# Attention, Fourier mixing and a feed-forward layer on one core: the second feed-forward product of the last three chunks as seven quarter products

## The chip, the core and the metric

One core of a Trainium2 chip runs the whole program. The metric is the device time of one execution in microseconds; lower is better. The engines are TensorE (PE in the profile; its weight loads are PEld), VectorE (DVE), ScalarE (ACT), GpSimd (POOL) and SyncE (SP), which here only starts transfers.

## What is computed

Eight sequences of 576 tokens, 8 heads of 64. All is float32.

```
a    = softmax(phi)                      # phi: 8, 8, 576, 32
k_m  = a^T k ;  v_m = a^T v              # 32 memory slots per head
attn = softmax(q k_m^T / 8) v_m
x    = heads side by side                # 8, 576, 512
u    = x + real(fft over tokens and over the 512 features of x)
un   = (u - mean) / sqrt(var + 1e-6)
out  = u + max(un @ w_ch1, 0) @ w_ch2    # w_ch1 512 x 2048, w_ch2 2048 x 512
```

## The kernel before

The 4608 tokens are 36 tiles of 128, taken in 18 chunks of two tiles (`CH = 2`). A generator, `background`, makes the rows of u of each batch: pooling weights, memories, scores, spectrum and the mixes (`mix_m`, `mix_x`, `add_mix`), which write u into a ring of eight tiles. `advance` runs it some steps further while the ring has room. `norm_chunk` normalises a chunk (ScalarE, VectorE, GpSimd), splits it into two float16 parts in `ud` and turns it with a transposing transfer on SP.

The feed-forward layer of a chunk goes in eight units (`NW = 8`), each of 256 hidden features (`UB = 2` blocks of 128). Float32 factors are two float16 parts, a high and a low one, and a product is three matmuls: high by high, high by low, low by high.

- `ffn1(c, unT, j, hs)` is the first product of a unit: 2 blocks x 4 x 3 = 24 matmuls of 256 columns (two tiles of 128 tokens), issued by the helper at line 288, into one PSUM bank `ph` (two buffers). ScalarE writes the high part of max(., 0) to the ring `hring` (line 864), VectorE the low part (line 865).
- `ffn2(c, j, hs, po)` is the second product: 2 blocks x 2 token tiles x 3 = 12 matmuls of 512 columns (line 874), with the hidden activations as the stationary operand and `w2s` as the moving one, added over all units into two PSUM banks `po`, one per token tile (pool `ps2`, two buffers).
- `finish(c, po)` adds u to each of the two banks on VectorE (line 886) and writes the tile out on SP (line 887).

The main loop goes over n, the units of chunks 1 to 17 in order: `ffn2` of unit n, then `run_ffn1(n + NHS)`, which emits first products up to seven units ahead (`NHS = 7`), then a step of the background; after a chunk's last unit `finish`, then the background until the tiles of chunk c + 2 are made, then the norm of chunk c + 2. This is the order of emission. A planner puts the instructions of each engine into their final order: it takes what was emitted earlier first, and what is emitted later where the earlier can't run yet by its own timing of the kernel. On the chip each engine then works through its list in order.

Of the buffers, `stg`, `rawt`, `phs`, `et`, `aeo`, `attnT`, `aring`, `vh`, `at` and `elt` belong to the background; after its last step they are not used.

Of the kernel before, what the change touches and what calls it, by code (L numbers as in the profile page):

```python
# [10 lines left out]
F32 = mybir.dt.float32  # L11
F16 = mybir.dt.float16
# [3 lines left out]
AF = mybir.ActivationFunctionType  # L16
ALU = mybir.AluOpType
# [3 lines left out]
P = 128  # L21
B, H, S, D, M = 8, 8, 576, 64, 32
NG = H // 2
DM = H * D
# [13 lines left out]
CH = 2  # L38
NU = 8
NHS = 7  # L40
# [8 lines left out]
BN = 2  # L49
UB = 2  # L50
NW = NF // UB
UW = UB * DM
EB = 14
L2 = [2, 4, 6]
# [4 lines left out]

HEADS = [0, 1, 2, 3, 7, 6, 5, 4]
SLOT = np.concatenate([np.arange(256), 511 - np.arange(256)])

# [69 lines left out]
def kernel(  # L134
# [39 lines left out]
    cout = small[:, 713:714]  # L174
# [17 lines left out]
    hring = const.tile([P, NW, 2, 4, P], F16, name="hring")  # L192
# [24 lines left out]
        nc.gpsimd.memset(t, 0.0)  # L217
    scratch = const.tile([P, 400], F32, name="scratch")
    share = const.tile([P, 2 * NJ], F32, name="share")
    rings, taken = {}, [0]  # L220

    def tiny(tag, n, bufs=2):
# [603 lines left out]
    def h_slot(c, j):  # L826
        return hring[:, (4 + c * NW + j) % NW]

# [17 lines left out]
    def ffn1(c, unT, j, hs):  # L846

        ph = ps1.tile([P, UB, CH, P], F32, tag="h", name=f"ph_{c}_{j}")
        mm = groups()
        for f in range(UB):  # L850
            i = 0
            for k in range(NK):
                for lw, lu in ((0, 0), (0, 1), (1, 0)):
                    mm(
                        ph[:, f],
                        lhsT=w1t[:, j, lw, k, f * P : (f + 1) * P],
                        rhs=unT[:, lu, :, k],
                        start=(i == 0),
                        stop=(i == 3 * NK - 1),
                    )  # L860
                    i += 1
        h = h_slot(c, j)
        phv = ph.rearrange("p f t c -> p (f t) c")
        nc.scalar.activation(h[:, 0], phv, AF.Relu)  # L864
        nc.vector.scalar_tensor_tensor(  # L865
            out=h[:, 1], in0=phv, scalar=0.0, in1=h[:, 0], op0=ALU.max, op1=ALU.subtract
        )
        hs.append(h)

    def ffn2(c, j, hs, po):  # L870
        for f in range(UB):
            for t in range(CH):
                for i, (lh, lw) in enumerate(((0, 0), (0, 1), (1, 0))):
                    nc.tensor.matmul(  # L874
                        po[t],
                        lhsT=hs[j][:, lh, f * 2 + t],
                        rhs=w2s[:, j * UB + f, lw, :],
                        start=(j == 0 and f == 0 and i == 0),
                        stop=(j == NW - 1 and f == UB - 1 and i == 2),
                    )  # L880

    def finish(c, po):
        for t in range(CH):
            idx = CH * c + t
            u = us.pop(idx)
            nc.vector.scalar_tensor_tensor(out=u, in0=po[t], scalar=cout if c else 0.5, in1=u, op0=ALU.mult, op1=ALU.add)  # L886
            nc.sync.dma_start(out=out[idx], in_=u)
# [110 lines left out]
    marks = {}  # L998
    us = {}
    n_tiles = B * S // P  # L1000
    n_chunks = n_tiles // CH
# [171 lines left out]
    def run_ffn1(upto):  # L1173
        nonlocal ahead
        while ahead < min(upto, n_steps):
            c, j = divmod(ahead, NW)
            ffn1(c, unTs[c], j, hs[c])
            ahead += 1
# [4 lines left out]
    for n in range(NW, n_steps):  # L1183
        c, j = divmod(n, NW)
        if j == 0:
            po = [ps2.tile([P, 512], F32, tag="o", name=f"po_{c}_{t}") for t in range(CH)]
        ffn2(c, j, hs[c], po)
        run_ffn1(n + NHS)
        if j < NW - 1:
            advance(CH * c, steps=1)  # L1190
        else:
            finish(c, po)
            if c + 2 < n_chunks:
                advance(CH * (c + 1), CH * (c + 3))
                unTs[c + 2] = norm_chunk(c + 2)


# [62 lines left out]
```

## Time and profile before

| | us |
|---|---|
| median of 3 runs | 943.62 (942.4 to 962.26) |
| the profiled execution | 943.25 |
| its span, first to last instruction | 941.4 |
| TensorE busy | 931.6 |
| VectorE busy | 548.0 |
| ScalarE busy | 459.6 |
| GpSimd busy | 217.5 |

The span is what the profile shows; the execution's own time is 1.85 us longer. Matmuls are pipelined and their ends are modelled, so what one matmul costs is read from how many stand in a stretch of known length, and not from the duration of one (379 ns for one of 512 columns). Lines of the kernel are given as L874.

### The profile page before, as it was taken

What the parts mean: (1) busy time and instruction counts of PE and PEld (TensorE: products, weight loads), DVE (VectorE), ACT (ScalarE), POOL (GpSimd) and SP (SyncE); (2) the same over time, 40 slices, a digit from 0 to 9 for tenths busy, and PEclk for the clock granted to TensorE, in tenths of its full rate; (3) what the DMA queues carried; (4) which work ended last, traced back from release to release, by engine and by line L of the source; (5) the groups of instructions that cost most, each with busy time, mean ns of one, the idle gap of its engine ahead of it and who ended that gap; (6) DMA issues with size and microseconds to landing.
All of it is one profiled execution on the core that took longest, in us unless ns stands there. A gap on an engine that the chain in (4) does not pass through costs nothing.

```text
span 941.4 us, 18994 instructions
## 1 busy us (share of the span) xinstructions
PE 931.6 (99%) x7820; PEld 666.2 (71%) x7820; DVE 548.0 (58%) x1271; ACT 459.6 (49%) x920; POOL 217.5 (23%) x255
## 2 busy tenths in 40 slices
PE   9999899999999999999999999999999999999998
PEld 8977577676777777676767767777776767666664
DVE  5989957576656666667514766667656675221111
ACT  5668858655465536554514554656446444311110
POOL 1313424142212314223100331323122231200000
PEclk9999899999999999999999999999999999999999
DMA  9957521642235412553104531373124211110000
GB/s 328 383 217 245 184 85 24 124 123 68 53 75 123 105 42 46 141 111 93 24 23 86 115 103 42 59 162 98 26 68 85 72 25 47 23 46 23 1 24 22
DMA packets 115959, 88.09 MB, mean 94 GB/s; under 512 B 100384, under 2 KB 100384, under 8 KB 113824
## 3 DMA queue, kind: packets, MB, share of 16 engines
q1 hardware_dynamic: 115872, 86.87, 34.7%
q8 instruction: 61, 1.00, 0.4%
q14 instruction: 26, 0.21, 0.1%
HBM read 58.15 MB, written 9.44 MB: 72 GB/s over the span
## 4 chain that ended last, share of the span: by engine, by line
PE 88%; DVE 3%; ACT 1%; issue 1%; POOL 0%; DVEq 0%; ACTq 0%
PE ph L288 38%; PE po L874 37%; PE pm L288 2%; PE pp_t L288 2%; PE px_t L288 2%; PE psc L288 1%; PE po L838 1%; PE pa L684 1%; DVE w2s L930 1%; PE ph L821 1%; PE pv L657 1%; PE pp_t L727 1%; PE pf L362 1%; DVE w1t L930 0%; ACT elt L941 0%
## 5 line engine op out<-in xcount | busy, mean ns | idle before, releaser
L288 PE MATMUL ph<-unring,w1t 128*128 128x256 f16 x3264 | 388.9, 273 | 0.0
L874 PE MATMUL po<-w2s,hring 128*128 128x512 f16 x1632 | 378.8, 379 | 0.0
L288 PEld LDWEIGHTS <-w1t 128*128 128x128 f16 x3264 | 315.0, 98 | 64.4 <-issue 3.3
L874 PEld LDWEIGHTS <-hring 128*128 128x128 f16 x1632 | 156.8, 98 | 158.0 <-issue 0.4
L865 DVE SCALAR_TENSOR_TENSOR hring<-ph,hring 128x512 f16<-128x512 f32 x136 | 93.1, 685 | 155.4 <-ACT hring L864 154.8
L864 ACT ACTIVATE hring<-ph 128x512 f16<-128x512 f32 x136 | 80.3, 591 | 161.3 <-PE ph L288 160.9
L592 POOL TENSOR_TENSOR aring<-aring,scratch 128x384 f32<-128x384 f32 x28 | 23.3, 833 | 212.2 <-DVE scratch L590 208.6
L787 POOL TENSOR_TENSOR scratch<-scratch,small 128x1 f32<-128x1 f32 x36 | 21.7, 608 | 168.2 <-DVE scratch L786 135.1
L288 PEld LDWEIGHTS <-stg 128*128 128x128 f16 x1152 | 44.8, 98 | 8.4
L586 ACT ACTIVATE aring<-aring,scratch 128x384 f32<-128x384 f32 x24 | 14.7, 612 | 71.0 <-DVE aring L585 71.0
L808 POOL TENSOR_TENSOR ud<-un,ud 128x1024 f16<-128x1024 f32 x17 | 36.2, 2129 | 29.6 <-ACT ud L807 27.7
L509 POOL TENSOR_TENSOR stg<-rawt,stg 128x640 f16<-128x640 f32 x12 | 17.7, 1475 | 90.2 <-ACT rawt L508 90.2
L838 PE MATMUL po<-w2s,hring 128*128 128x512 f32 x64 | 32.8, 637 | 4.3 <-ACT hring L824 4.2
L611 ACT CAST aeo<-eo 128x384 f16<-128x384 f32 x30 | 15.3, 511 | 41.4 <-DVE eo L608 41.4
L886 DVE SCALAR_TENSOR_TENSOR uring<-po,small,uring 128x512 f32<-128x512 f32 x34 | 24.0, 742 | 17.6 <-PE po L874 17.6
L576 DVE TENSOR_REDUCE scratch<-psc 128x12 f32<-128x384 f32 x32 | 17.6, 549 | 28.5 <-PE pm L288 16.1
L763 DVE SCALAR_TENSOR_TENSOR uring<-px_t,scratch,share 128x256 f32<-128x256 f32 (+1 forms) x80 | 33.9, 475 | 0.2 <-PE px_t L288 0.2
L602 POOL TENSOR_TENSOR aring<-aring 128x128 f32<-128x128 f32 x56 | 32.8, 605 | 2.1
L604 DVE TENSOR_TENSOR eo<-aring 128x128 f32<-128x128 f32 x29 | 29.5, 1018 | 5.9 <-POOL aring L602 5.9
L288 PE MATMUL pm<-et,stg 128*128 128x64 f16 (+1 forms) x740 | 32.0, 195 | 0.0
L821 PE MATMUL ph<-unring,w1t 128*128 128x256 f32 x128 | 32.0, 395 | 0.0
L749 DVE SCALAR_TENSOR_TENSOR share<-pp_t,scratch,small 128x257 f32<-128x257 f32 (+1 forms) x48 | 21.0, 480 | 18.1 <-ACT small L746 18.0
(263 smaller groups left out, 1212.3 us busy)
## 6 DMA issues: line engine op xcount, KB each, us to landing
out<-uring SPq DMA_DIRECT2D x36, 256.0 KB, 2.1
rawt<-in_raw SPq DMA_DIRECT2D x13, 640.0 KB, 4.9
stg<-in_raw SPq DMA_DIRECT2D x13, 640.0 KB, 4.8
stg<-in_w SPq DMA_DIRECT2D x7, 1024.0 KB, 6.0
rawt<-in_raw SPq DMA_DIRECT2D x15, 384.0 KB, 3.3
stg<-in_raw SPq DMA_DIRECT2D x15, 384.0 KB, 3.1
phs<-in_raw SPq DMA_DIRECT2D x28, 160.0 KB, 3.8
w2s<-in_w SPq DMA_DIRECT2D x4, 1024.0 KB, 10.8
```

The source lines that it names most:

```text
L288: m = nc.tensor.matmul(out, lhsT=lhsT, rhs=rhs, start=start, stop=stop)
L592: eng.tensor_tensor(out=a, in0=a, in1=sm.unsqueeze(2).to_broadcast([P, 12, M]), op=ALU.mult)
L602: eng.tensor_tensor(out=a2[:, i : i + 4], in0=a[:, 0:4], in1=a[:, 4:8], op=op)
L604: nc.vector.tensor_tensor(out=eo[:, 1:3, 0], in0=ap[:, 1:3, 0], in1=ap[:, 1:3, 1], op=ALU.add)
L763: nc.vector.scalar_tensor_tensor(out=u[rows, hs], in0=px[rows, hs], scalar=igx[rows], in1=tm[rows, w * NJ + half : w * NJ + half + 256], o ...
L808: marks[f"ul{c}"] = nc.gpsimd.tensor_tensor(out=ud[:, 1], in0=un, in1=ud[:, 0], op=ALU.subtract)
L821: nc.tensor.matmul(ph, lhsT=w[:, k, f * P : (f + 1) * P], rhs=unTs[0][:, k], start=(k == 0), stop=(k == NK - 1))
L838: nc.tensor.matmul(po[t], lhsT=h[:, f, t], rhs=w[:, f], start=(j == 0 and f == 0), stop=(j == NW - 1 and f == UB - 1),)
L864: nc.scalar.activation(h[:, 0], phv, AF.Relu)
L865: nc.vector.scalar_tensor_tensor(out=h[:, 1], in0=phv, scalar=0.0, in1=h[:, 0], op0=ALU.max, op1=ALU.subtract)
L874: nc.tensor.matmul(po[t], lhsT=hs[j][:, lh, f * 2 + t], rhs=w2s[:, j * UB + f, lw, :], start=(j == 0 and f == 0 and i == 0), stop=(j == NW ...
L886: nc.vector.scalar_tensor_tensor(out=u, in0=po[t], scalar=cout if c else 0.5, in1=u, op0=ALU.mult, op1=ALU.add)
```

## The change

In chunks 15, 16 and 17 (`C0 = 15`) the second product of a unit, a 2 x 2 block matrix of activations (two token tiles by two hidden blocks) by a 2 x 2 block matrix of weights (two hidden blocks by two halves of 256 output columns), is made from seven block products in place of eight (Winograd's form of Strassen's scheme). Every product is three float16 matmuls of 256 columns, so 21 in place of 12 of 512.

- `ffn1_sums` takes the place of the two activations in `ffn1`: ScalarE writes the four blocks in float32, VectorE makes four sums of blocks, ScalarE the high parts of the seven blocks used, VectorE the low ones. They go to seven slots (`NS = 7`) in buffers of the background and of `hring`.
- `prepare_sums(j)` makes the four sums of weight blocks of unit j once, in chunk 14, on GpSimd, through one float32 buffer `t_sum` (in `at`); ScalarE and VectorE split them into `t_slots[j]`.
- The seven products are added over all units in PSUM, in four banks, two products to a bank but for p4. In the last chunk, from unit 4 on, p1, p6, p7 and p5 come first for all units, then p2, p4 and p3.
- `finish_sums` puts the products together into the four quarters.
- First products are emitted six units ahead (`NS - 1`) from chunk 15 on, and at the end of chunk 13 the background is emitted to its end.

```diff
+FIRST, SECOND = ["p1", "p6", "p7", "p5"], ["p2", "p4", "p3"]
...
+    t_slots = [stg[:, i, k * 2048 : (k + 1) * 2048] for i in (0, 2) for k in range(2)]
+    t_slots += [rawt.bitcast(F16)[:, k * 2048 : (k + 1) * 2048] for k in range(2)]
+    t_slots += [stg[:, 1, k * 2048 : (k + 1) * 2048] for k in range(2)]
...
+    s_slots = [flat(phs, "t g c").bitcast(F16), flat(et, "g l t c"), flat(aeo, "l t e h c"), flat(attnT, "g t c")]
+    s_slots += [flat(hring[:, i : i + 2], "a l f c") for i in (4, 6, 0)]
...
+    sums = [flat(aring, "a t m")[:, : 8 * P], flat(vh, "l k c").bitcast(F32)]
...
+    t_sum = flat(at, "a c").bitcast(F32)[:, : 2 * DM].rearrange("p (f c) -> p f c", f=UB)
...
+        if c >= C0:
+            hs.append(ffn1_sums(c, j, ph))
+            return
         h = h_slot(c, j)
...
+    def prepare_sums(j):
+        w, t, N = w2s[:, j * UB : (j + 1) * UB], t_sum, DM // 2
+        nc.gpsimd.tensor_tensor(out=t, in0=w[:, :, 0], in1=w[:, :, 1], op=ALU.add)
+        b11, b12, b21, b22 = (t[:, f, n * N : (n + 1) * N] for f in range(2) for n in range(2))
+        nc.gpsimd.tensor_tensor(out=b11, in0=b12, in1=b11, op=ALU.subtract)
+        nc.gpsimd.tensor_tensor(out=b12, in0=b22, in1=b12, op=ALU.subtract)
+        nc.gpsimd.tensor_tensor(out=b22, in0=b22, in1=b11, op=ALU.subtract)
+        nc.gpsimd.tensor_tensor(out=b21, in0=b21, in1=b22, op=ALU.subtract)
+        hi, lo = (t_slots[j][:, l].rearrange("p b c -> p (b c)") for l in range(2))
+        tf = t.rearrange("p f c -> p (f c)")
+        nc.scalar.copy(out=hi, in_=tf)
+        nc.vector.tensor_tensor(out=lo, in0=tf, in1=hi, op=ALU.subtract)
+
+    def ffn1_sums(c, j, ph):
+        m = (c - C0) * NW + j
+        a, h = sums[m % 2], s_slots[m % NS]
+        nc.scalar.activation(a[:, 0:4], ph.rearrange("p f t c -> p (f t) c"), AF.Relu)
+        for o, x, y, op in ((6, 1, 0, ALU.subtract), (4, 0, 2, ALU.add), (5, 2, 6, ALU.subtract), (7, 3, 5, ALU.subtract)):
+            nc.vector.tensor_tensor(out=a[:, o], in0=a[:, x], in1=a[:, y], op=op)
+        nc.scalar.copy(out=h[:, 0], in_=a[:, 1:8])
+        nc.vector.tensor_tensor(out=h[:, 1], in0=a[:, 1:8], in1=h[:, 0], op=ALU.subtract)
+        return h
+
+    def sums_banks(c):
+        banks = [ps2.tile([P, 512], F32, tag="o", name=f"po_{c}_{i}") for i in range(2)]
+        banks += [psg.tile([P, 512], F32, tag="g", name=f"po_{c}_{2 + i}") for i in range(2)]
+        names = ("p1", "p2"), ("p6", "p7"), ("p5", "p3"), ("p4",)
...
+    def ffn2_sums(j, h, po, names):
...
+        for n in names:
+            a, b = factors[n]
+            for i, (la, lb) in enumerate(((0, 0), (0, 1), (1, 0))):
+                with tc.issue_after(marks["ps"].ins) if i == 0 and "ps" in marks else nullcontext():
+                    m = nc.tensor.matmul(
+                        po[n],
+                        lhsT=h[:, la, a],
+                        rhs=b[lb],
...
+    def finish_sums(c, po):
...
+        def add(o, p, x):
+            nc.vector.scalar_tensor_tensor(out=o, in0=po[p], scalar=cout, in1=x, op0=ALU.mult, op1=ALU.add)
+
+        nc.scalar.activation(c1, po["p1"], AF.Copy, scale=cout)
+        add(x1, "p6", c1)
+        add(x2, "p7", x1)
+        add(x3, "p5", x1)
+        nc.gpsimd.tensor_tensor(out=u1[:, lo], in0=u1[:, lo], in1=c1, op=ALU.add)
+        nc.vector.tensor_tensor(out=u2[:, hi], in0=u2[:, hi], in1=x2, op=ALU.add)
+        add(u2[:, hi], "p5", u2[:, hi])
+        nc.vector.tensor_tensor(out=u1[:, hi], in0=u1[:, hi], in1=x3, op=ALU.add)
+        nc.vector.tensor_tensor(out=u2[:, lo], in0=u2[:, lo], in1=x2, op=ALU.add)
+        add(u1[:, lo], "p2", u1[:, lo])
+        add(u2[:, lo], "p4", u2[:, lo])
+        nc.sync.dma_start(out=out[CH * c], in_=u2)
+        add(u1[:, hi], "p3", u1[:, hi])
+        nc.sync.dma_start(out=out[CH * c + 1], in_=u1)
...
+        if c >= C0:
+            late = c == n_chunks - 1 and j >= NW // 2
+            ffn2_sums(j, hs[c][j], po, FIRST if late else FIRST + SECOND)
+            if late and j == NW - 1:
+                for p in SECOND:
+                    for i in range(NW // 2, NW):
+                        ffn2_sums(i, hs[c][i], po, [p])
+        else:
+            ffn2(c, j, hs[c], po)
+        run_ffn1(n + (NHS if n + NHS <= C0 * NW else NS - 1))
+        if c == C0 - 1:
+            prepare_sums(j)
...
-            finish(c, po)
+            (finish_sums if c >= C0 else finish)(c, po)
             if c + 2 < n_chunks:
-                advance(CH * (c + 1), CH * (c + 3))
+                advance(CH * (c + 1), n_tiles if c == C0 - 2 else CH * (c + 3))
                 unTs[c + 2] = norm_chunk(c + 2)
```

## Rows read from the trace of the kernel before

**Rows 1.** The page's first part: of each engine the busy time, its share of the span and its instructions.
```profile
PE 931.6 (99%) x7820; PEld 666.2 (71%) x7820; DVE 548.0 (58%) x1271; ACT 459.6 (49%) x920; POOL 217.5 (23%) x255
```

**Rows 2.** The page's second part: the span in 40 equal slices, TensorE's busy share in tenths and its granted clock in tenths of full speed.
```profile
PE   9999899999999999999999999999999999999998
PEclk9999899999999999999999999999999999999999
```

**Rows 3.** Busy time of each engine between the finishes of chunks 13, 14, 15 and 16 (776.5, 825.0, 866.7 and 908.4 us): the stretch, its length, per engine busy us and instructions, granted clock, DMA share, GB/s.
```profile
776.50:825.00 48.50, 48.50 (x388) 34.66 (x386) 19.66 (x51) 18.20 (x39) 9.49 (x8) 1.00 0.15 35
825.00:866.70 41.70, 41.70 (x289) 28.16 (x288) 6.94 (x10) 4.78 (x8) 0.00 (x0) 1.00 0.11 26
866.70:908.40 41.70, 41.70 (x289) 28.18 (x288) 6.95 (x11) 4.78 (x8) 0.00 (x0) 1.00 0.04 13
```

**Rows 4.** The chain that ended last, in order of time: start, length, engine, tile, line. Unit 0 of chunk 15 begins its second product at 828.26, unit 7 at 864.73; the last line is the end of the chain on TensorE.
```profile
825.64 2.62 PE ph L288 x24
828.26 2.59 PE po L874 x12
...
864.73 2.59 PE po L874 x12
...
919.42 2.62 PE ph L288 x24
922.04 14.91 PE po L874 x69
```

**Rows 5.** Groups of ScalarE instructions by line and shape, whole span: shapes, count, busy us, mean ns, idle time before them and what ended it.
```profile
L864 ACT ACTIVATE hring<-ph 128x512 f16<-128x512 f32 x136 | 80.3, 591 | 161.3 <-PE ph L288 160.9
...
L807 ACT CAST ud<-un 128x1024 f16<-128x1024 f32 x17 | 17.7, 1043 | 25.8 <-DVE un L788 21.1 <-DMA unring<-ud 4.7
L561 ACT ACTIVATE stg<-rawt,scratch 128x768 f16<-128x768 f32 x12 | 11.1, 924 | 0.0
L824 ACT ACTIVATE hring<-ph 128x256 f32<-128x256 f32 x16 | 6.0, 376 | 2.2 <-PE ph L821 2.0
```

**Rows 6.** The same for GpSimd; the last line is of the view of one tile (`aring`), with duration in ns as minimum, median and maximum, then first and last start.
```profile
L808 POOL TENSOR_TENSOR ud<-un,ud 128x1024 f16<-128x1024 f32 x17 | 36.2, 2129 | 29.6 <-ACT ud L807 27.7 <-PE pl L362 1.9
L592 POOL TENSOR_TENSOR aring<-aring,scratch 128x384 f32<-128x384 f32 x28 | 23.3, 833 | 212.2 <-DVE scratch L590 208.6 <-DVE small L257 3.6
L612 POOL TENSOR_TENSOR aeo<-eo,aeo 128x256 f16<-128x256 f32 x30 | 21.2, 706 | 27.1 <-ACT aeo L611 27.1
...
L602 POOL TENSOR_TENSOR aring<-aring x56: 449/457/1053, 86.8 to 773.5; 128x128 f32<-128x128 f32 x56
```

**Rows 7.** The same for VectorE; the last two lines are of the view of one tile (`aring`), over the whole span and over 700 to 800 us, with duration in ns as minimum, median and maximum, then first and last start.
```profile
L763 DVE SCALAR_TENSOR_TENSOR uring<-px_t,scratch,share 128x256 f32<-128x256 f32 x64 | 26.9, 474 | 0.2 <-PE px_t L288 0.2
L585 DVE TENSOR_TENSOR aring<-psc,scratch 128x384 f32<-128x384 f32 x30 | 16.6, 555 | 0.3
L956 DVE SCALAR_TENSOR_TENSOR w1t<-w1t,small 128x1024 f16<-128x1024 f32 x5 | 6.6, 1324 | 1.1 <-ACT w1t L951 1.0
...
L604 DVE TENSOR_TENSOR eo<-aring x29: 273/866/1473, 26.3 to 774.0; 128x128 f32<-128x128 f32 x29
L604 DVE TENSOR_TENSOR eo<-aring x4: 862/1320/1470, 728.5 to 774.0; 128x128 f32<-128x128 f32 x4
```

**Rows 8.** Timeline of GpSimd and VectorE at 743.9 to 745.4 us: start, length, engine, line, operation; the idle time before it in brackets.
```profile
743.93 1.40 POOL L509 TENSOR_TENSOR stg<-rawt,stg 128x640 f16<-128x640 f32 x1
744.00 1.47 DVE L604 TENSOR_TENSOR eo<-aring 128x128 f32<-128x128 f32 x1 [0.37 <-POOL aring L602]
745.29 0.83 POOL L600 TENSOR_TENSOR ahring<-aring,ahring 128x320 f16<-128x320 f32 x1
745.39 0.94 DVE L608 TENSOR_TENSOR eo<-aring 128x192 f32<-128x192 f32 x1
```

**Rows 9.** Timeline around one bank of `pm` at 759 to 765 us. Thirty matmuls fill it, the first fifteen its columns 0 to 63, the others columns 64 to 127; L534 reads columns 0 to 63.
```profile
759.30 0.75 PE L288 MATMUL pm<-et,stg 128*128 128x64 f16 x20
...
762.87 0.86 DVE L613 SCALAR_TENSOR_TENSOR aeo<-aeo,small,eo 128x128 f16<-128x128 f16 x1 [0.58 <-ACT aeo L611]
...
764.00 0.45 PE L288 MATMUL pm<-et,stg 128*128 128x64 f16 x10
...
764.49 0.22 DVE L534 TENSOR_TENSOR scratch<-pm,small 128x64 f32<-128x64 f32 x1 [0.16 <-PE pm L288]
```

**Rows 10.** Timeline of the end of the background: the last mix's matmuls, which read `at`, and the norm of chunk 15 on GpSimd and SP.
```profile
794.17 2.13 POOL L808 TENSOR_TENSOR ud<-un,ud 128x1024 f16<-128x1024 f32 x1 [1.74 <-ACT ud L807]
794.63 1.48 PE L288 MATMUL pp_t<-vh,at 128*128 128x257 f16 x12
...
796.32 1.89 SPq L271 DMA_TRANSPOSE unring<-ud  x1
```

**Rows 11.** Timeline of the finish of chunk 14, and of chunk 17 at the end of the program.
```profile
822.89 2.75 PE L874 MATMUL po<-w2s,hring 128*128 128x512 f16 x12
...
825.03 1.41 DVE L886 SCALAR_TENSOR_TENSOR uring<-po,small,uring 128x512 f32<-128x512 f32 x2 [0.62 <-PE po L874]
825.48 2.78 PE L288 MATMUL ph<-unring,w1t 128*128 128x256 f16 x24
...
933.75 3.83 PE L874 MATMUL po<-w2s,hring 128*128 128x512 f16 x17
...
936.97 1.41 DVE L886 SCALAR_TENSOR_TENSOR uring<-po,small,uring 128x512 f32<-128x512 f32 x2 [13.57 <-PE po L874]
```

More of the change, by code (lines that the diff above doesn't have):

```diff
@@ L51 @@
 NW = NF // UB
+C0 = 15
+NS = 7
 UW = UB * DM
@@ L219, with flat @@
     share = const.tile([P, 2 * NJ], F32, name="share")
+    def flat(t, names):
+        return t.rearrange(f"p {names} -> p ({names})")
+    t_slots = [stg[:, i, k * 2048 : (k + 1) * 2048] for i in (0, 2) for k in range(2)]
+    t_slots += [rawt.bitcast(F16)[:, k * 2048 : (k + 1) * 2048] for k in range(2)]
+    t_slots += [stg[:, 1, k * 2048 : (k + 1) * 2048] for k in range(2)]
+    t_slots = [t.rearrange("p (l b c) -> p l b c", l=2, b=4) for t in t_slots]
+    s_slots = [flat(phs, "t g c").bitcast(F16), flat(et, "g l t c"), flat(aeo, "l t e h c"), flat(attnT, "g t c")]
+    s_slots += [flat(hring[:, i : i + 2], "a l f c") for i in (4, 6, 0)]
+    s_slots = [t[:, : 14 * P].rearrange("p (l b c) -> p l b c", l=2, b=7) for t in s_slots]
+    sums = [flat(aring, "a t m")[:, : 8 * P], flat(vh, "l k c").bitcast(F32)]
+    sums = [t.rearrange("p (b c) -> p b c", b=8) for t in sums]
+    t_sum = flat(at, "a c").bitcast(F32)[:, : 2 * DM].rearrange("p (f c) -> p f c", f=UB)
     rings, taken = {}, [0]
@@ new lines, in sums_banks, with plain, summed @@
+    def sums_banks(c):
+        banks = [ps2.tile([P, 512], F32, tag="o", name=f"po_{c}_{i}") for i in range(2)]
+        banks += [psg.tile([P, 512], F32, tag="g", name=f"po_{c}_{2 + i}") for i in range(2)]
+        names = ("p1", "p2"), ("p6", "p7"), ("p5", "p3"), ("p4",)
+        return {n: banks[i][:, k * 256 : (k + 1) * 256] for i, p in enumerate(names) for k, n in enumerate(p)}
+    def ffn2_sums(j, h, po, names):
+        def plain(f, n):
+            return [w2s[:, j * UB + f, l, n * 256 : (n + 1) * 256] for l in range(2)]
+        def summed(b):
+            return [t_slots[j][:, l, b] for l in range(2)]
+        factors = {
+            "p1": (0, plain(0, 0)),
+            "p6": (4, summed(3)),
+            "p7": (5, summed(1)),
+            "p5": (3, summed(0)),
+            "p2": (2, plain(1, 0)),
+            "p4": (1, summed(2)),
+            "p3": (6, plain(1, 1)),
+        }
+        for n in names:
[6 more added lines that the diff above has]
+                        rhs=b[lb],
+                        start=(j == 0 and i == 0 and n in ("p1", "p6", "p5", "p4")),
+                        stop=(j == NW - 1 and i == 2),
+                        skip_group_check=True,
+                    )
+            marks["ps"] = m
@@ new lines, in finish_sums @@
+    def finish_sums(c, po):
+        u2, u1 = us.pop(CH * c), us.pop(CH * c + 1)
+        lo, hi = slice(0, 256), slice(256, 512)
+        c1, x1 = share[:, 0:256], share[:, 256:512]
+        x2, x3 = (elt.rearrange("p l c -> p (l c)").bitcast(F32)[:, i * 256 : (i + 1) * 256] for i in range(2))
+        def add(o, p, x):
[14 more added lines that the diff above has]
+        nc.sync.dma_start(out=out[CH * c + 1], in_=u1)
@@ L1185 @@
         if j == 0:
-            po = [ps2.tile([P, 512], F32, tag="o", name=f"po_{c}_{t}") for t in range(CH)]
-        ffn2(c, j, hs[c], po)
-        run_ffn1(n + NHS)
+            po = sums_banks(c) if c >= C0 else [
+                ps2.tile([P, 512], F32, tag="o", name=f"po_{c}_{t}") for t in range(CH)
+            ]
+        if c >= C0:
[10 more added lines that the diff above has]
+            prepare_sums(j)
         if j < NW - 1:
```

## The prediction

> **What bounds the kernel now.** I read the engines' shares first: TensorE 931.6 of 941.4 us, at full granted clock in nearly every slice [rows 1, 2]. A busy TensorE is not yet a bound one, so I asked for the stretches between the finishes of chunks 13, 14, 15 and 16. There TensorE is busy in every microsecond, while VectorE has 6.9, ScalarE 4.8 and GpSimd 0 of 41.7 us in chunk 15 [rows 3]. The chain that ended last is there an unbroken alternation: 24 first-product matmuls in 2.62 us, 12 second-product matmuls in 2.59 us, one pair per unit of work, 5.21 us, and at the end 69 second-product matmuls in 14.91 us [rows 4]. So TensorE's own work sets the time of the last three chunks, and what is taken from it there comes off the end, as long as nobody makes it wait.
>
> All sums start from the profiled execution: 943.25 us, span 941.4, so 1.85 us lie around the span; the median of the runs is 943.62, 0.37 more.
>
> **1. The second product in seven products.** Before: 12 matmuls of 512 columns per unit, 2.59 us, 216 ns each. After: 7 quarter products of 3 terms, 21 matmuls of 256 columns. The row nearest to these is the first product, also 256 columns with another stationary block every time: 2.62/24 = 109 ns [rows 4]. 21 x 109.2 = 2.29 us, 0.30 us less per unit; 24 units (chunks 15 to 17) give -7.14 us. One matmul of 512 columns costs 216, two of 256 cost 218, so the half width gives away 1%. If the halves were exact (108 ns), it would be -7.7; I see no way to more than 109.2, since these rows already carry a weight load for every matmul.
>
> The Trainium skill has a rule against this change: "TensorE: Matmul & The Clock Gate", section Back-to-back issue gap, gives a stream of weight loads and matmuls 131 ns at 512 columns and 81 ns at 128. An estimate from that page, about 98 ns at 256, would make 21 of them 2.06 us against 1.57 us for the twelve, and the change 11.7 us slower. The trace has 216 and 109 ns and decides; those are the same section's figures for one isolated matmul.
>
> **2. The sums of the hidden activations**, per unit. ScalarE's activation now writes float32 (as before 0.6 us) and adds an 896-wide copy: between the 768-wide row, 0.92, and the 1024-wide, 1.04 [rows 5], 0.98. So 1.6 us of 4.91 us per unit. VectorE gives up one instruction and gets four 128-wide subtractions and an 896-wide one. Alone: 4 x 0.273 (the minimum) and 1.2, a little under the 1.32 of 1024 columns, 2.3 us; with GpSimd at work 4 x 1.32 (the median of the last four) and 1.4, 6.7 us [rows 7]. The 2.3 fits the pitch. At 6.7 VectorE falls 1.8 us behind per unit, for as long as GpSimd works on part 3 (some 70 us, 14 units): 25 us, against a lead of six units, 29 us. The lead just covers it; I take 0.
>
> **3. The weights' sums in chunk 14**, per unit of eight, in one chain over one buffer (in `at`): GpSimd 1024 wide, 2.13, and four times 256 wide, each 0.65 (between 0.46 at 128, the median, and 0.83 at 384; the 256-wide row says 0.71 with another output) [rows 6]; ScalarE's copy 1.04 [rows 5]; VectorE's subtraction 1.32 [rows 7]; 0.2 of handing over. That is 7.3 us per unit, 58 us, beside TensorE. It can't begin before the last mix has read `at`, 796.1 us [rows 10]. The change has the mixes emitted ahead of the norm of chunk 15, so I put that at 791, and add 3 us for this norm's GpSimd work (one instruction of 2.13 and its small ones). Set j is there at 794 + c(j+1), c being the length of the cycle. It is wanted when unit j of chunk 15 begins: now at 828.26 + 5.21 j [rows 4]; with one unit less of lead and the shorter unit 825.6 + 4.91 j, that is 860.0 for the last one. Set 7 is the critical one: 794 + 8c. TensorE can be kept fed for another 2.6 us by one first-product unit that is moved ahead, so it stands still for 8c - 68.6 us.
>
> What is c? VectorE's and GpSimd's instructions get into each other's way: a 128-wide subtraction takes 0.27 alone and 1.47 beside GpSimd's 1.40 us, and the next one again ends with GpSimd's next [rows 7, 8]. The Trainium skill ("SBUF — State Buffer", section SBUF: two separate sides) calls this an exclusive lock: a VectorE instruction with two SBUF inputs and a GpSimd one that reads SBUF don't run at once. All of the sums' instructions in parts 2 and 3 on VectorE are of that kind. By the rows, then, c lies between 7.3 (nobody waits) and 10.7 (all 3.4 us that VectorE spends per cycle on the sums of 1.5 units come on top). GpSimd is idle for a third of the cycle, and some of VectorE's work falls there: I take 8.5, where the stall is 0. Ends: 0 and +17.
>
> **4. Finishing a chunk.** Before, two VectorE instructions of 0.74 us. After, one on ScalarE (0.38, 256 wide [rows 5]), one on GpSimd, and ten on VectorE, 0.41 to 0.47 each (between 384 wide, 0.56, and 256 wide, 0.47 [rows 7]). What matters is when they can start. A bank of PSUM is not read while products are still being added into its other half: in [rows 9] VectorE sat idle before 762.87 and again before 764.49, though the half that it wanted had got its fifteen matmuls by 760.05; it started once the other half's last ten, from 764.00, were over. Quarter p1 shares a bank with p2, p5 with p3.
>
> At the very end: p2 is complete 24 matmuls, 2.6 us, before the last matmul, which is p3's. In these 2.6 us fit ScalarE's copy, p6, p7, the adds that need only these, and p2. Behind the last matmul stay p5 twice, the add of x3 and p3, 4 x 0.45 = 1.8 us, and perhaps p4: 2.3. Before, 0.8 us lay there (last matmul over at 937.6, adds at 938.4 [rows 11]). The transfer behind it is the same. So +1.5 us, between +1.0 and +1.7. Were the bank not waited for, only p3 would stay, -0.3.
>
> Between chunks 15, 16 and 17: the next chunk's first matmul wants the bank of p1 and p2. Before, it was free 0.95 us after the chunk's last matmul and wanted 2.6 us after it (one first-product unit lies between) [rows 11]. Now p2's add is the eighth or so of the ten, 3.5 us after; with the sums of a unit in between, 5.7. So 0.9 to 3.1 us of standing still per boundary, or 0 if another first-product unit is put ahead. I take 0.5 each, +1.0; ends 0 and +6.2.
>
> **5. The rest.** The last background work emitted earlier and one unit less of lead move work and add none; the transposing transfers of the norms stay on SP, and chunk 15's is issued (796.32 [rows 10]) perhaps 3 us later, behind which there are second products to do. No transfer is added. The first products with float32 output into two small buffers wait at most for VectorE, part 2. I take 0.
>
> Sum: -7.14 + 1.5 + 1.0 + 0 = -4.6; 943.25 - 4.6 = 938.6, against the median 939.0. I say **938.9**.
>
> **Rivals.**
> *The chain of part 3 is late* (slower than before). Place: TensorE waits in chunk 15 for t_slots 5 to 7. Price: 8 us per microsecond of c above 8.6; from c = 9.2 the whole gain is gone, at 10.7 the time is 938.6 + 17 = 956. For it: the rows on both engines' mutual waiting, one buffer, and GpSimd's norms of chunks 16 and 17 between. Against: 23 us of slack for the first set and GpSimd's idle third. Chance 0.2.
> *The finish eats it.* The boundaries cost 3.1 us each and the tail 1.7: 943.25 - 7.14 + 1.7 + 6.2 = 944.0, no change. For it: ten instructions in the place of two on one queue, and the sums queued among them. Against: first-product units can fill. Chance 0.13.
> *The full gain.* No wait for a bank, tail -0.3, boundaries filled: 943.25 - 7.14 - 0.3 = 935.8. Against it stands [rows 9]. Chance 0.07.
> *Forecast*, 937 to 942: 0.6.
>
> **How the numbers follow.** About 2% (19 us) is what a measurement of this kernel can tell from no change; the whole of the term that gains is 7.1 us, so faster by over 2% has 0.01. Slower by over 2% needs c above 11.6 or something that I don't see: 0.03. Within: 0.96. The range takes in the full gain, the eaten one and the lower half of the late chain: 935.5 to 947. The likeliest case's own range is 937 to 942.
>
> **What would show it.** Right: second-product matmuls of 256 columns, 504 of them, 109 ns apart; the alternation in chunks 15 and 16 with a period of 4.9 us; no idle time of TensorE there; some 2.3 us from the last matmul to the last add. Late chain: gaps before the summed products p6, p7, p5, p4 of chunk 15's units 5 to 7, released by VectorE's subtraction in `prepare_sums`, whose cycle is over 9 us. Eaten by the finish: gaps of 1 to 3 us at the heads of chunks 16 and 17, released by VectorE. Wrong altogether: a matmul pitch other than 109 ns, or a different course of the time before 776 us.

## The result and the profile after

The changed kernel takes **947.93 us** (median of five runs) against 942.67 us for the kernel before: ratio 1.0051, 95% interval [1.0040, 1.0062]. Forecast was 938.9, range 935.5 to 947.0. A gain of some 4 us was expected, and a loss of 5 came; the measured time lies 0.9 us above the range. Some executions of most kernels here take 16 to 22 us longer than the rest; the medians count them, the ratios leave them out, and the profile of `finish_act` below is of such a one, so that only its waits are used.

The profiled execution took 948.03 us, span 946.3 (before 943.25 and 941.4). The page's first part and the rows of TensorE in its second, which answer to [rows 1, 2]:

```profile
PE 927.6 (98%) x8036; PEld 688.8 (73%) x8036; DVE 617.9 (65%) x1399; ACT 490.0 (52%) x955; POOL 265.1 (28%) x298
...
PE   9999899999999999999999999999999999989997
...
PEclk9999899999999999999999999999999999989999
```

TensorE is busy for less time than before (927.6 against 931.6), and a slice near the end has fallen below nine tenths in both rows. So work was saved, and more time was lost by waiting. TensorE's waits from 800 us on (engine, tile, line, released by, us in total, times, longest); before there was none from 700 us to the end:

```profile
PE po L953 <- DVE uring L991: 5.2, 1, 5.2
PE po L953 <- ACT stg L913: 2.0, 1, 2.0
```

The granted clock and the other engines' work, in stretches around the two waits (columns as in [rows 3]):

```profile
823.60:831.40 7.80, 2.62 (x24) 2.20 (x23) 6.67 (x11) 2.96 (x4) 3.69 (x3) 0.90 0.00 0
831.40:836.00 4.60, 4.56 (x22) 3.17 (x22) 4.33 (x8) 2.74 (x4) 2.19 (x2) 0.50 0.33 118
836.00:840.00 4.00, 4.00 (x36) 3.44 (x35) 1.39 (x4) 0.60 (x1) 3.70 (x3) 0.93 0.00 0
840.00:866.00 26.00, 26.00 (x240) 23.31 (x239) 21.81 (x26) 9.23 (x12) 17.53 (x16) 1.00 0.11 21
866.00:876.00 10.00, 8.01 (x74) 7.03 (x73) 7.19 (x13) 5.19 (x8) 3.27 (x4) 1.00 0.00 1
```

VectorE has 21.8 us of work in the 26 us from 840 on, where it had 6.9 in 41.7 [rows 3], and GpSimd 17.5 where it had none. Behind the first wait the granted clock is 0.50, that is 1.2 in place of 2.4 GHz, for 4.6 us. TensorE itself around both waits, which answers to [rows 4, 11]:

```profile
823.43 2.78 PE L305 MATMUL ph<-unring,w1t 128*128 128x256 f16 x24
831.44 0.80 PE L953 MATMUL po<-w2s,phs 128*128 128x256 f16 x3 [5.22 <-DVE uring L991]
...
834.17 0.84 PE L953 MATMUL po<-w2s,phs 128*128 128x256 f16 x3
...
843.76 0.49 PE L953 MATMUL po<-w2s,aeo 128*128 128x256 f16 x3
...
848.67 0.49 PE L953 MATMUL po<-w2s,attnT 128*128 128x256 f16 x3
...
871.46 0.27 PE L953 MATMUL po<-stg,phs 128*128 128x256 f16 x1 [1.99 <-ACT stg L913]
```

Unit to unit it is 848.67 - 843.76 = 4.91 us, as forecast (before 5.21). But chunk 15's first second-product matmul waits 5.22 us for L991, VectorE's pass over chunk 14's banks. What VectorE and GpSimd did then (L922 are the four sums of the activations and L924 their split into float16 parts, L905 to L910 the weights' sums and L914 their split):

```profile
822.63 1.54 DVE L922 TENSOR_TENSOR aring<-aring 128x128 f32<-128x128 f32 x4
825.23 1.09 DVE L924 TENSOR_TENSOR aeo<-aring,aeo 128x896 f16<-128x896 f32 x1 [1.06 <-ACT aeo L923]
826.24 1.22 DVE L914 TENSOR_TENSOR stg<-at,stg 128x1024 f16<-128x1024 f32 x1
827.37 3.35 DVE L922 TENSOR_TENSOR vh<-vh 128x128 f32<-128x128 f32 x4
830.65 1.40 DVE L991 SCALAR_TENSOR_TENSOR uring<-po,small,uring 128x512 f32<-128x512 f32 x2
...
827.53 2.12 POOL L905 TENSOR_TENSOR at<-w2s 128x1024 f32<-128x1024 f16 x1 [4.24 <-DVE stg L914]
829.73 0.85 POOL L907 TENSOR_TENSOR at<-at 128x256 f32<-128x256 f32 x1
830.66 0.73 POOL L908 TENSOR_TENSOR at<-at 128x256 f32<-128x256 f32 x1
```

Before, the pass started at 825.03, as soon as its first bank was complete, and the next first product followed chunk 14's last matmul at 825.48 [rows 11]. Now, with one first-product unit less ahead, chunk 14's last matmul is over 2 us earlier (the next first product starts at 823.43), but the pass starts only at 830.65, 7.2 us later. It stands in VectorE's queue behind the sums and the split of one unit's activations, the split of weight set 2 (1.22 us), which follows ScalarE's copy of that set at 825.10, and four more small sums. These four take 3.35 us beside GpSimd; without GpSimd's sums the same four take 1.02 us (experiment no_weight_sums). So the stretched sums right ahead of the pass are 2.3 of the 7.2 us, and the rest is what else stands in the queue.

The weight sets. ScalarE's copy of the sets, from set 0 to set 7 without 4 and 5, and GpSimd's last sum of sets 2 and 7:

```profile
800.80 1.03 ACT L913 CAST stg<-at 128x1024 f16<-128x1024 f32 x1
813.47 1.04 ACT L913 CAST stg<-at 128x1024 f16<-128x1024 f32 x1
825.10 1.04 ACT L913 CAST stg<-at 128x1024 f16<-128x1024 f32 x1
833.76 1.04 ACT L913 CAST stg<-at 128x1024 f16<-128x1024 f32 x1 [1.51 <-POOL at L910]
...
859.98 1.05 ACT L913 CAST stg<-at 128x1024 f16<-128x1024 f32 x1 [0.47 <-POOL at L910]
870.37 1.04 ACT L913 CAST stg<-at 128x1024 f16<-128x1024 f32 x1
...
821.84 1.45 POOL L910 TENSOR_TENSOR at<-at 128x256 f32<-128x256 f32 x1
867.10 1.45 POOL L910 TENSOR_TENSOR at<-at 128x256 f32<-128x256 f32 x1
```

The end of the program, on TensorE and VectorE:

```profile
940.55 0.49 PE L953 MATMUL po<-w2s,aeo 128*128 128x256 f16 x3
...
942.72 0.48 DVE L970 SCALAR_TENSOR_TENSOR uring<-po,small,uring 128x256 f32<-128x256 f32 x1
```

From the last matmul's end to the last add's: 943.20 - 941.04 = 2.16 us, before 0.8.

**The sum.** The first 130 us vary from execution to execution: the first chunk's finish starts between 128.2 and 130.9 us in the profiles shown in this document, and all that follows is shifted by as much. So I compare what lies behind that point: 941.4 - 130.3 = 811.1 us before, 946.3 - 130.9 = 815.4 after, +4.3. The terms: products 504 x 109.2 ns - 288 x 216 ns = -7.2; tail (from the last matmul's end on) +1.4; wait for the bank +5.2; wait for set 7 +2.0; clock (4.56 us of work at 0.50, 4.0 at 0.93: 2.3 + 0.3) +2.6. Together +4.0; 0.3 us is left.

### The profile page after: what moved, and what is told of

Same layout as the page of the kernel before. It is cut to its first block, busy times and chain, and to the rows that moved or that the text cites. A ratio compares the mean times of both kernels' runs of the same rounds, so it can differ in the third digit from the quotient of the medians.

```text
span 946.3 us, 19659 instructions
## 1 busy us (share of the span) xinstructions
PE 927.6 (98%) x8036; PEld 688.8 (73%) x8036; DVE 617.9 (65%) x1399; ACT 490.0 (52%) x955; POOL 265.1 (28%) x298
## 4 chain that ended last, share of the span: by engine, by line
PE 80%; DVE 7%; ACT 3%; POOL 2%; issue 1%; ACTq 0%; DVEq 0%
PE ph L305 34%; PE po L894 29%; PE po L953 4%; PE pm L305 2%; PE pp_t L305 2%; PE px_t L305 2%; PE psc L305 1%; DVE vh L922 1%; PE po L855 1%; PE pa L701 1%; DVE w2s L1035 1%; PE ph L838 1%; PE pv L674 1%; PE pp_t L744 1%; PE pf L379 1%
## 5 line engine op out<-in xcount | busy, mean ns | idle before, releaser
L894 PE MATMUL po<-w2s,hring 128*128 128x512 f16 x1344 | 314.0, 379 | 0.0
L894 PEld LDWEIGHTS <-hring 128*128 128x128 f16 x1344 | 128.8, 98 | 127.5 <-issue 0.4
L885 DVE SCALAR_TENSOR_TENSOR hring<-ph,hring 128x512 f16<-128x512 f32 x112 | 76.5, 683 | 61.0 <-ACT hring L884 60.3
L884 ACT ACTIVATE hring<-ph 128x512 f16<-128x512 f32 x112 | 65.9, 589 | 59.3 <-PE ph L305 59.0
L617 POOL TENSOR_TENSOR ahring<-aring,ahring 128x320 f16<-128x320 f32 x29 | 23.9, 823 | 25.5 <-ACT ahring L616 25.5
```

The lines of the kernel that those rows point to most:

```text
L617: nc.gpsimd.tensor_tensor(out=ahl[:, :, 64:128], in0=av[:, 0:5], in1=ahl[:, :, 0:64], op=ALU.subtract)
L885: nc.vector.scalar_tensor_tensor(out=h[:, 1], in0=phv, scalar=0.0, in1=h[:, 0], op0=ALU.max, op1=ALU.subtract)
L894: nc.tensor.matmul(po[t], lhsT=hs[j][:, lh, f * 2 + t], rhs=w2s[:, j * UB + f, lw, :], start=(j == 0 and f == 0 and i == 0), stop=(j == NW ...
```

## Experiments

All edits are made in the changed kernel; the code shows the lines that matter of each, with `...` for others. "Behind the start" is the span of the profile less the start of the first finish, as above (before 811.1, after 815.4); the last column is TensorE's waits from 700 us on.

| kernel | median us | ratio to before [95%] | behind the start | waits of TensorE, us |
|---|---|---|---|---|
| after | 947.93 | 1.0051 [1.0040, 1.0062] | 815.4 | 5.2 bank, 2.0 set |
| own_banks | 947.20 | 1.0046 [1.0029, 1.0063] | 815.4 | 5.2 bank, 2.2 set |
| two_buffers | 945.25 | 1.0026 [1.0016, 1.0037] | 814.9 | 2.9 bank, 2.7 attention, 1.0 ScalarE |
| both | 943.77 | 1.0013 [1.0001, 1.0024] | 814.8 | 2.5 bank, 2.7 attention, 1.0 ScalarE |
| no_weight_sums | 936.75 | 0.9938 [0.9921, 0.9955] | 805.7 | none |
| held_banks | 947.32 | 1.0051 [1.0036, 1.0066] | 815.1 | 5.9 sets |
| held_both | 941.32 | 0.9985 [0.9975, 0.9995] | 810.2 | 2.7 attention |
| best3 | 941.54 | 0.9986 [0.9976, 0.9995] | 810.4 | 2.7 attention |
| finish_act | 947.01 | 1.0049 [1.0032, 1.0065] | - | 3.5 transfer, 2.3 sets, 1.3 bank |
| sums_on_dve | 937.29 | 0.9947 [0.9929, 0.9964] | 806.3 | 0.7 bank |
| late_both | 945.97 | 1.0034 [1.0019, 1.0049] | 815.9 | 6.7 in six places |
| late_best | 946.03 | 1.0031 [1.0020, 1.0043] | 813.8 | 6.4 in six places |
| dve_best | 937.87 | 0.9949 [0.9933, 0.9964] | 805.8 | none |

Three theories. **1**: the wait for the pass over chunk 14 is the loss. **2**: the weight sets come too late and set the pace. **3**: GpSimd's sums and VectorE's two-input instructions hold each other up, and both waits are consequences.

**own_banks**

```
-        banks = [ps2.tile(...) for i in range(2)] + [psg.tile(...) for i in range(2)]
+        banks = [psg.tile(...) for i in range(4)]      # chunk 15 only
```

> Chunk 15's seven sums get four PSUM banks that the finish of chunk 14 does not read, so nothing waits for that finish; all else is as changed. Theory 1 (that wait, 5.2 us, and the half clock behind it, 2.6 us, are the loss): 7.8 us less, 940. Theory 2 (the weights' sums come one set per 9 to 10 us and would be the next to wait for): set 7 is still split at about 871 us and is now wanted at 861, so some 10 us of waits for sets 5 to 7 take the place of 7.8 and the 2.0 that were there; the time stays within 1 us of the change, 947 to 949.

Measured 947.20, and the bank wait is still there, 5.23 us. The experiment missed its aim. The likely reason is that a tile of the other pool was again given a bank that chunk 14 had used; the profile names tiles and not banks, so this is not shown, but the same edit with the banks taken earlier (held_banks) does remove the wait. own_banks says nothing on the theories.

**two_buffers**

```
+    t_sum2 = ...                       # a second float32 buffer, in w2s
...
-        w, t, N = w2s[...], t_sum, DM // 2
+        w, t, N = w2s[...], (t_sum, t_sum2)[j % 2], DM // 2
```

> The weights' sums go through two float32 buffers by turns, so GpSimd need not wait for ScalarE and VectorE of the set before. Theory 2: the wait for set 7 (2.0 us) goes, the wait for the finish of chunk 14 stays: 946. Theory 1 alone says the same. Theory 3 (VectorE is late because of GpSimd's denser work): sets come every 6 to 7 us, VectorE's 128-wide sums are held even more often, and the finish of chunk 14 comes 1 to 3 us later: 947 to 949, with the wait for it above 5.2.

Measured 945.25. The set wait is gone and the bank wait down to 2.9 us, but two new waits of 2.7 and 1.0 us stand in their place:

```profile
PE po L954 <- DVE uring L992: 2.9, 1, 2.9
PE pa L694 <- DVE aeo L631: 2.7, 1, 2.7
PE ph L306 <- ACT vh L921: 1.0, 1, 1.0
```

The second buffer is free while `at` is still in use, so the sets that use it are made early (the first copy is at 761.7 us), beside the last attention tiles, and TensorE waits there. Theory 3 had expected a longer bank wait; it became shorter, with half of the sets moved away from it.

**both** (the two edits above)

> Own banks for chunk 15 and two buffers together. Theories 1 and 2 together (the two waits are all that stands between the change and its prediction): both waits and the half clock go, 9.8 us less: 938. If VectorE as such is too slow beside GpSimd (theory 3), TensorE waits next for the sums of the activations themselves: 941 to 945, with gaps released by the 896-wide subtraction.

Measured 943.77. As own_banks took no wait away, this is two_buffers once more: 814.8 us against 814.9 behind the start. The medians differ by 1.5 us, and the intervals of the two ratios overlap.

**no_weight_sums** (GpSimd's five instructions per set left out; the split reads another block)

```
-        nc.gpsimd.tensor_tensor(out=t, in0=w[:, :, 0], in1=w[:, :, 1], op=ALU.add)
-        ... four nc.gpsimd.tensor_tensor(...) of 256 columns
-        tf = t...
+        tf = w1t[:, NW]...      # float32 of the same size
```

> GpSimd's five instructions per set are left out: the split reads some other float32 block in place of the weights' sums; VectorE's and ScalarE's part of each set stays, and the banks are as changed. Theory 3 (GpSimd's work holds VectorE's two-input instructions, and so the finish of chunk 14 behind them): 128-wide sums take 0.27 us in place of 0.4 to 0.85, the finish of chunk 14 runs within 2 us of its last matmul, no wait for sets: 9 to 10 us less, 938. If the order of VectorE's queue alone makes the finish late: the wait of some 4 to 5 us and the half clock stay, 945 to 946.

Measured 936.75: 11.2 us less than the changed kernel. No wait of TensorE is left, and the clock is full:

```profile
815.00:840.00 25.00, 25.00 (x218) 21.08 (x216) 15.81 (x33) 9.65 (x13) 1.51 (x1) 1.00 0.06 22
...
822.54 1.02 DVE L916 TENSOR_TENSOR vh<-vh 128x128 f32<-128x128 f32 x4
823.47 1.40 DVE L985 SCALAR_TENSOR_TENSOR uring<-po,small,uring 128x512 f32<-128x512 f32 x2
```

The four sums ahead of the pass take 1.02 us, and the pass starts at 823.47 in place of 830.65 us (1.9 of the 7.2 come from the start). But the edit took away more than GpSimd's work. The splits no longer wait for `at`: the last of the eight starts at 772.6 us, where the changed kernel copies and splits the sets between 800 and 873. So this run shows that the loss comes with making the weight sets where the change makes them. It does not show by itself that GpSimd's side of that is the cause; sums_on_dve, further down, keeps the sets at their place (its splits start between 798.4 and 850.6). The run also gives the size of what the change saves when nothing waits: 805.7 - 811.1 = -5.4 us, where products and tail make -7.2 + 1.4 = -5.8.

**held_banks** (own_banks, and chunk 15's banks taken early, so that none can be chunk 14's)

```
+            if j == 4:                       # in chunk 14
+                ahead_banks.append(sums_banks(C0))
+                for p in ("p1", "p6", "p5", "p4"):
+                    nc.tensor.matmul(ahead_banks[0][p], lhsT=unread[:, :P], rhs=unread, ...)
```

> The changed kernel, but chunk 15's four banks are asked for in chunk 14's fifth unit and taken at once by one 256-column product each (of constants, overwritten later), so that chunk 15's first product cannot be given a bank that chunk 14's last pass empties. Adds four products, 0.4 us. Theory 1 (the wait for the pass over chunk 14, 5.2 us, and the half clock behind it, 2.6 us, are the loss): 947.9 - 7.8 + 0.4 = about 940.5. Theory 2 (weight sets late): the sets are made in the same time as before, set 5 to 7 are then wanted some 5 to 8 us earlier than they are ready, the wait only moves from the first product to these sets: about 947. Theory 3 (GpSimd's work holds VectorE's queue) as theory 2, since nothing of that work is taken away: 945 to 948.

Measured 947.32. The bank wait is gone, and nothing is won: chunk 15 begins its second product at 825.97 in place of 831.44, and then waits for sets 5, 6 and 7, which are ready when they were before.

```profile
PE po L954 <- ACT stg L913: 3.4, 2, 2.4
PE po L954 <- DVE rawt L914: 1.0, 1, 1.0
PE po L954 <- DVE stg L914: 0.9, 1, 0.9
PE po L954 <- ACT rawt L913: 0.6, 1, 0.6
```

The clock is 0.66 from 860 to 870 us. Theory 1 falls as a cause by itself: the bank wait had only covered the late sets.

**held_both** (held_banks and two_buffers)

> As the kernel with chunk 15's banks held from chunk 14's fifth unit, and the sums of every other weight set made in a second buffer, so that a set's first sum need not wait for the split of the set before. Adds four products, 0.4 us. Theory 1: the bank wait is away, about 940.5. Theory 2: the bank wait and most of the wait for sets are away (sets come every 6 to 7 us in place of 8.7): 938 to 942. Theory 3: GpSimd's 1.25 us per sum and VectorE's stretched sums remain, only packed into less time; VectorE is then behind by itself and product one waits on its activation sums: 942 to 945.

Measured 941.32, 1.4 us below the kernel before. Both waits are gone; what is left stands earlier, beside the attention, with its clock:

```profile
781.70 0.42 PE L694 MATMUL pa<-ct,aeo 128*128 128x290 f16 x1 [2.71 <-DVE aeo L631]
...
780.00:785.00 5.00, 3.31 (x25) 2.94 (x26) 3.17 (x5) 2.46 (x5) 2.12 (x3) 0.66 0.45 138
```

Theories 1 and 2 together account for it: the two waits are in parallel, and taking away either leaves most of the loss. Theory 3's number (942 to 945) was too high. Whether the new wait, beside the attention, is of its kind is not shown.

**best3** (held_both, sets 0 to 2 made at the end of chunk 13, p5 and p4 sharing a bank)

```
+                if c == C0 - 2:
+                    for i in range(3):
+                        prepare_sums(i)          # all three in t_sum2
...
-        names = ("p1", "p2"), ("p6", "p7"), ("p5", "p3"), ("p4",)
+        names = ("p1", "p2"), ("p6", "p7"), ("p5", "p4"), ("p3",)
```

> Chunk 15's banks held from chunk 14's fifth unit, two buffers for the sums, and the first three weight sets made a chunk earlier (at the end of chunk 13), so that GpSimd's work in chunk 14 falls by 3/8; besides, the last products pair as p5 with p4 in one bank and p3 alone, so that the last four additions need fewer waits on a bank under writing. All work of the changed kernel is done, plus four products (0.4 us). Theory 1: as with held banks and pairs, 940.5 - 1 = about 939.5. Theory 2 and 3: sets ready with lead and VectorE's queue free at the end of chunk 14, no wait of TensorE from 820 us on: 936.7 (the kernel without GpSimd's sums) + 0.4 - 1 = 936 to 938.

Measured 941.54, not 936 to 938. From 815 us on TensorE waits for nothing, but the same 2.7 us at the attention remain, since the sums made earlier lie beside it.

**finish_act** (the pass over chunk 14 by ScalarE, its add by GpSimd)

```
+                nc.scalar.activation(e, po[t], AF.Copy, scale=cout)        # e = un[:, t]
+                nc.gpsimd.tensor_tensor(out=u, in0=u, in1=e, op=ALU.add)
```

> The changed kernel, but the pass over chunk 14's two banks is done by ScalarE (0.6 us each) with the sum to the residual by GpSimd from SBUF, in place of VectorE behind its queue. Nothing else is changed. Theory 1 and theory 3 (the pass was late because VectorE's queue ahead of it was held): the 5.2 us wait for it falls to below 1.5 us; the sets come no sooner, so part of it returns as a wait for set 5 to 7: 943 to 946. Theory 2 (the sets set the pace): no gain, 947 to 948, since GpSimd has two more sums of 512 columns to make.

Measured 947.01. The bank wait falls from 5.2 to 1.3 us, as theories 1 and 3 say; waits for sets take 2.3; and the edit made a wait of its own, 3.5 us for a transposing transfer whose norm needs the block `un` that I had used. It doesn't tell the theories apart.

**sums_on_dve** (one edit: the weights' sums on VectorE in place of GpSimd)

```
-        nc.gpsimd.tensor_tensor(...)      # all five of prepare_sums
+        nc.vector.tensor_tensor(...)
```

> The changed kernel with one edit: the five sums of each weight set are made by VectorE in place of GpSimd, in the same buffer and the same order. VectorE gets some 2.3 to 4 us more work in each of the eight sets; GpSimd has none of it left. Theory 3 (the two engines hold each other up while both read with two inputs, and the pass over chunk 14 stands behind that): without the second engine each sum takes its undisturbed time, a set 5 to 7 us in place of 8.7, the wait for the pass over chunk 14 falls below 2 us and the wait for set 7 goes: 940 to 943. Rival (VectorE simply has too much work in chunk 14, whoever else works): 8 times 3 us more of it, the pass over chunk 14 comes later still: 950 or more.

Measured **937.29**, ratio 0.9947 [0.9929, 0.9964]: 10.6 us less than the changed kernel, 5.4 less than the kernel before, by giving the busier engine the work of the idler one. Theory 3 had said 940 to 943. One wait of 0.72 us is left. The groups of the four sums from 795 to 880 us, first in the changed kernel, then here (shapes, count, busy us, mean ns, idle time before):

```profile
L922 DVE TENSOR_TENSOR aring<-aring 128x128 f32<-128x128 f32 x27 | 14.6, 576 | 0.3
L922 DVE TENSOR_TENSOR vh<-vh 128x128 f32<-128x128 f32 x24 | 14.5, 641 | 2.8 <-ACT vh L920 2.6
```

```profile
L922 DVE TENSOR_TENSOR aring<-aring 128x128 f32<-128x128 f32 x32 | 8.2, 283 | 2.1 <-ACT aring L920 2.0
L922 DVE TENSOR_TENSOR vh<-vh 128x128 f32<-128x128 f32 x30 | 7.5, 284 | 3.8 <-ACT vh L920 3.7
```

Each takes 0.28 us here and about 0.61 on average beside GpSimd. The weights' sums themselves are cheaper on VectorE too: 1.22 us for 1024 columns and 0.42 to 0.48 on average for 256, against 2.12 to 2.90 and 0.73 to 1.45 on GpSimd. Set 7's copy starts at 849.5 in place of 870.4 (2.1 of it from the start). The rival, too much work for VectorE, falls. The edit does two things at once, though: the engines no longer block each other, and each set's sums are made in less time. No run has the one without the other.

**late_both** (held_both, but no sum issued ahead of set 0's)

```
+        with tc.issue_after(marks["set0"].ins) if j else nullcontext():
+            m = nc.gpsimd.tensor_tensor(out=t, in0=w[:, :, 0], in1=w[:, :, 1], op=ALU.add)
```

> Chunk 15's banks held from chunk 14's fifth unit and the sums made in two buffers in turn, as in the kernel that came to 941.3, but no sum of a later set may be issued ahead of set 0's, whose buffer comes free only with the end of the attention work near 800 us. So the sums that stood at 762 to 791 us, beside the last attention tile (where TensorE then waited 2.7 us for VectorE's passes and had a clock of 0.91), move behind it. If that wait and that clock are what was left of the loss: 941.3 - 2.7 - 1.6 = about 937. If not, and the sums in the shorter time make VectorE late in chunk 15: 941 to 944, with waits of TensorE for sets or activation sums at 830 to 860 us.

Measured 945.97: 9 us above the first case, 2 above the second. The wait at the attention is gone, but the sums now come in pairs without a break, and VectorE stands behind them (VectorE's rows, then GpSimd's):

```profile
829.11 5.06 DVE L925 TENSOR_TENSOR vh<-vh 128x128 f32<-128x128 f32 x3
834.10 0.74 DVE L995 SCALAR_TENSOR_TENSOR uring<-po,small,uring 128x512 f32<-128x512 f32 x1
...
828.13 3.03 POOL L907 TENSOR_TENSOR at<-w2s 128x1024 f32<-128x1024 f16 x1 [3.84 <-DVE stg L917]
831.13 2.17 POOL L907 TENSOR_TENSOR w2s<-w2s 128x1024 f32<-128x1024 f16 x1
833.26 0.77 POOL L910 TENSOR_TENSOR at<-at 128x256 f32<-128x256 f32 x1
```

Three sums of 0.28 us take 5.06 us, and GpSimd ends three instructions in this time, at 831.16, 833.30 and 834.03. The pass behind them, with one input from PSUM, takes its usual 0.74 us beside GpSimd. This is where the blocking of theory 3 shows most plainly: less idle time for GpSimd, more waiting for VectorE.

**late_best** (late_both, p5 and p4 sharing a bank)

> As the kernel with held banks, two buffers and no sum ahead of set 0's, and besides the fourth and fifth product share a bank and the third is alone in one, so that the last chunk's closing additions are not in a row behind one bank. Tail of the changed kernel 2.16 us behind the last product, of the kernel before 0.8: if the pairing is the cause, 1.2 us less than its twin: about 936; if the closing additions are bound by VectorE, the same as its twin.

Measured 946.03, no different. Its tail is 1.95 us against 2.15 in its twin: the pairing is worth 0.2 us there, not 1.2 (behind the start the two profiles differ by 2.1 us, the medians not). The last three adds, 1.26 us in a row, are VectorE's own time.

**dve_best** (sums_on_dve, held_banks and that pairing)

> Sums of the weights on VectorE in one buffer, chunk 15's banks held from chunk 14's fifth unit, and the products paired as p5 with p4 and p3 alone. Theory 3: no engine holds the other, all sets in time and no wait for a bank: 936 to 939. Rival (too much work for VectorE in chunk 14): sets 5 to 7 late or the activation sums late, waits of TensorE of over 5 us in all: 943 or more.

Measured 937.87, TensorE without any wait; behind the start 805.8 us, 0.5 less than sums_on_dve, and by the medians the same. With the sums on VectorE, with or without the two other edits, the kernel is faster than before and than after.

## Why the prediction was wrong

**Part 1, the products: right.** 109 ns per matmul, 4.91 us per unit, -7.2 us. The sustained figures of the Trainium skill ("TensorE: Matmul & The Clock Gate", section Back-to-back issue gap), from which the prediction estimated a change 11.7 us slower, are not borne out: a matmul of 256 columns takes the measured 109 ns against that estimate's 98, and one of 512 took 216 before against the page's 131. That the time did go up has another cause.

**Part 4, the tail: right** (+1.4 against +1.5). The boundaries 15 to 16 and 16 to 17 cost 0 in place of +1.0: no wait stands at either. The one boundary that did cost, 14 to 15, I had not priced at all. There the pass is the old one, two instructions, and I looked only at the new finish of ten.

**Part 3, the failed step: "I take 8.5, where the stall is 0."** Set 7's copy starts at 870.37 and its split is over at 872.7; by the formula's start, 794, that is c = (872.7 - 794)/8 = 9.84. The formula then gives a stall of 8 x 9.84 - 68.6 = 10.1 us. Measured were 5.2 + 2.0 of waits and 2.6 of clock, 9.8 together, and 938.6 + 10.1 = 948.7 against 947.9 measured. So the rival "the chain of part 3 is late" came true, at about its own price; its chance of 0.2 was too low, and its range had been cut at 947.

Where c went wrong shows in the copies. From set 2 on to set 6 they are 8.7 to 8.9 us apart, near my 8.5. But sets 0 to 2 are 12.7 and 11.6 apart, and set 7 follows 10.4 us behind set 6: these three gaps are 9.2 us more than three times 8.5. The norms' GpSimd work, for which I had allowed 3 us once, lies three times among sets 0 to 2. And for sets 2 and 7 GpSimd was done (823.29 and 868.55) 1.8 us before the copy began (825.10 and 870.37), because the activations' copy stood ahead of it in ScalarE's queue; the prediction had only 0.2 us of handing over. I had both ends, 7.3 and 10.7, and let "GpSimd is idle for a third" pull the value to the end where nothing happens.

**Part 2, half right.** VectorE's sums were bounded by 2.3 and 6.7 us per unit, and the lead was to cover them. For the first products it did, as no matmul of theirs waited. But the lead covers only those who wait for the sums. The pass over chunk 14 stands in the same queue, behind them and behind the split of set 2, and has no lead; the 5.2 us fell there.

**The place of the loss.** The rival had put it at sets 5 to 7; in the changed kernel most of it shows at chunk 15's first matmul. Read from that profile alone, the bank seems the cause. held_banks shows that it is not by itself (947.3), held_both that the two waits cover each other (941.3), and no_weight_sums and sums_on_dve that all but 0.7 us of both goes when GpSimd has no sums to make (936.8, 937.3). How much of the lateness is blocking, and how much is that GpSimd needs longer for the same sums, these two runs leave open; that there is blocking, the rows show. [Rows 7, 8] had shown the pattern before: a 128-wide subtraction, 0.27 us at its shortest, took 1.47 beside a GpSimd instruction of 1.40. The Trainium skill says it as a rule ("SBUF — State Buffer", section Who interferes with whom): with two SBUF inputs against a GpSimd instruction that reads SBUF, the second to issue is blocked until the first is done. The rows agree: 0.28 us become up to 2.23 (the rows below, of the changed kernel; ns as minimum, median, maximum). They bear out the exception of that section too, an instruction with one SBUF input: the pass, with its other input from PSUM, kept its 0.74.

```profile
L922 DVE TENSOR_TENSOR aring<-aring x48: 277/285/2226, 809.1 to 926.1; 128x128 f32<-128x128 f32 x48
L922 DVE TENSOR_TENSOR vh<-vh x48: 276/285/2224, 816.9 to 931.0; 128x128 f32<-128x128 f32 x48
```

With the sums on VectorE the forecast's sum holds: -7.2 + 1.4 + 0.7 = -5.1, measured 806.3 - 811.1 = -4.8, and 937.3 us lies in the likeliest case's own range.

What was not tried by itself is the clock: that the half clock behind the 5.2 us costs 2.6 us is read from the rows, and no run kept TensorE busy through that wait. But the last wait ends with set 7's copy, so at full clock it would probably have been longer by as much: in held_banks the waits are others (5.9 us), the low clock lies elsewhere (0.66 from 860 to 870 us), and the time is the same.

## What to carry to other kernels

Where VectorE and GpSimd block each other, price a small VectorE instruction with two SBUF inputs at the length of the GpSimd instruction beside it (here 0.28 us became up to 2.23), and ask what stands behind it in the queue, not only who wants its result. An "idle" engine was no free place for such work; moving the sums to the busier one was worth 10.6 us. And when a wait in a profile is removed and nothing is won, look for a second one that it had covered before giving up on either.

## Not expected

- Waits of TensorE had different ends, even those near in length. The stretch behind the 5.2 us wait ran at 0.50; around the 2.0 us wait at 871 the clock stayed 1.00; the 2.7 us wait at 782 in held_both stands in a stretch of 0.66.
- The blocking goes both ways: GpSimd's 1024-wide add takes 2.12 us and, where an 896-wide split of VectorE's had started just before it, 2.90; its 256-wide ones take 0.73 to 1.45.
- A tile taken from another PSUM pool still waited 5.2 us for the pass over chunk 14 (own_banks). Taking it early (held_banks) ended that; taking it from elsewhere did not.
